# Gate steps by thirds and both all-reduces at their end, gated Wo columns on VectorE, a K row ahead of a scale part: one change to an adaLN attention block

## The chip, the cores and the metric

The kernel runs on one core of one Trainium2 chip. The metric is the device time of one execution in microseconds; lower is better. Of the kernel before there are three timed runs and one profiled execution.

## The reference

Two sequences of 256 tokens (512 rows) with 1152 channels. Everything arrives and leaves in bf16.

```python
B, N, D = (2, 256, 1152)
mod = (silu(c) @ w_mod).reshape(B, 6, 1, D)
shift_a, scale_a, gate_a = mod[:, 0], mod[:, 1], mod[:, 2]     # the other three are not used
h = layernorm(x) * (1 + scale_a) + shift_a
q, k, v = split(h @ wqkv, 3)
p = softmax(q @ k.T * D ** -0.5)                               # one head of 1152 channels
return x + gate_a * ((p @ v) @ wo)
```

## The kernel before, in words

1152 channels are nine tiles of 128 (`KT`), 512 tokens are four tiles of 128 (`TT`; two of each sequence), and most outputs are cut into chunks of 384 columns (`CW`). Weights are loaded by the SP queue in the order in which the code issues them; eight semaphores go round, so a load is issued only when the one eight places ahead of it has landed. Each engine's compute instructions run in the order in which the code calls them: the wrappers `vec`, `sca`, `ten` and `gps` record every call, and `pin` fixes that order at the end. Since the wrapper makes the call, the profile has nearly every instruction under one line, L85, and groups are told apart by the tile names. PSUM has eight banks: five called MM and one each of BA, BB and BC; `bank(..., where=...)` names one, and without `where` it takes the next of the ring.

**K, with the normalisation drawn through it.** Channels are the contraction, so x is centred (`centre`, with means from VectorE's `bn` or ScalarE's `act_mean`), transposed on TensorE (`transposes`, tile `tp`) and copied to `xcT` (`xcT_copy`). The scale of the first channel tiles comes from `scale_rows` on TensorE in three parts, PA (tiles 0 to 1), PB (2 to 4), PC (5 to 8): 9 rows of `wS` for each tile, into `psS`; `scale_open` starts each part with a matmul of ones by ones, so that the sum is 1 + scale, and `scale_out` copies it to `s1p`. `scaled` multiplies a row of `xcT` by it into `hTs`. K's nine output tiles: the first five are accumulated through all nine rows (`accs`; `k_part` and `k_step`, five matmuls a row), the other four take rows 0 and 1 in pairs (`pair_part`), are parked in SBUF (`held`) and are finished by `held_block(0)` to `held_block(3)`: seven matmuls each for rows 2 to 8 and an addition on VectorE. The inverse deviation `rstd` is made on GpSimd from the variances, spread over the partitions by a transpose and a matmul (`parts`, `pT3`, `masked`, `bc_ps`) and multiplied into all of `hTs` by VectorE (`normalised`, tile `hT`). Then the shift (`psH`, 36 matmuls in bank BB, turned into `shT`) is added to `hT` (`shifted`) by VectorE and ScalarE. The order is: `held_block(0)` and `(1)`, `psH`, `held_block(2)` and `(3)`; the last of them uses bank BB too.

**Q, scores, V.** Q takes nine rows of `wQ` (`psQ`), the scores of both sequences follow (`s_ps`), and then V in 12 groups of nine matmuls (`v_group`). The gate is not a matmul: VectorE accumulates silu(c) times `wG` in `gacc`, one partition a row of `w_mod`, in 9 steps for each sequence (`gate_steps`), first all of sequence 0 and then of sequence 1. `spread` sums over the partitions with one all-reduce on GpSimd for each sequence (`gate_bc`). VectorE makes the row maxima and the negated maxima (`scores`: `p_f`, `mx`, `nmx`), ScalarE the exponentials (`exps`), VectorE the division (`probs`, tile `pn`), and the DMA queue turns the result (`turn`, `pT`).

**Attention times V and Wo.** `pT` times `v_sb` gives `attnT`; the PSUM groups are cast by VectorE and ScalarE in turn. Then four row blocks of Wo, in chunks: VectorE multiplies a chunk by the gate (`ga`) and adds x (`o_sb`); the store follows. The last row block is cut finer. Its last 192 columns use `wo_last`, columns of Wo that GpSimd multiplied by the gate in nine steps, so that only x has to be added afterwards: by VectorE for 128 columns, and by an identity matmul on TensorE and a copy on ScalarE for the last 64.

Of the kernel before, what the change touches and what calls it, by code (L numbers as in the profile page):

```python
# [7 lines left out]
ACT = mybir.ActivationFunctionType  # L8
# [8 lines left out]
def kernel(  # L17
# [92 lines left out]
    def one(t):  # L110
        return slice(t * P, (t + 1) * P)
# [9 lines left out]
    ones_row = const.tile([1, 512], BF16)  # L121
    gps.memset(ones_row, 1.0)
# [5 lines left out]
    def mask_make():  # L128
        gps.memset(mask, 1.0)
        gps.affine_select(  # L130
            out=mask, in_=mask, compare_op=ALU.is_ge, fill=0.0, base=0,
            pattern=[[-3, TT], [0, P]], channel_multiplier=1,
        )
        gps.affine_select(
            out=mask, in_=mask, compare_op=ALU.is_ge, fill=0.0, base=2,
            pattern=[[3, TT], [0, P]], channel_multiplier=-1,
        )
# [18 lines left out]
    def load_s(part, k0, k1):  # L156
        load_mod(wS, 1, k0, k1, part[0] * P, part[1] * P)

    def load_k(k0, k1, c0=0, c1=D):
        spq.dma_start(out=wK[:, k0:k1, c0:c1], in_=wqkv_v[:, k0:k1, D + c0 : D + c1])  # L160
# [19 lines left out]
    load_k(3, 4)  # L180
    load_s(PC, 0, 4)
    load_s(PC, 4, KT)
    load_k(4, 5)
    load_k(5, 7)
# [3 lines left out]
    for k0, k1 in ((0, 2), (2, 5), (5, KT)):  # L188
        load_q(k0, k1)
# [16 lines left out]
    def silu_c():  # L206
        sca.activation(out=e_sb, in_=c_sb, func=ACT.Exp, scale=-1.0)
        gps.tensor_scalar_add(out=e_sb, in0=e_sb, scalar1=1.0)
        vec.reciprocal(out=r_sb, in_=e_sb)
        gps.tensor_tensor(out=scT_f.rearrange("p k b -> p b k"), in0=c_sb, in1=r_sb, op=ALU.mult)  # L210
        gps.tensor_copy(out=scT_rep, in_=scT_f.unsqueeze(2).to_broadcast([P, KT, NR // B, B]))
# [13 lines left out]
    def bn(t):  # L225
        st = small.tile([P, NCH, 6], F32, tag="stats", name="stats")
        for s in range(NCH):
            bn_part(t, st, s)
        mv = small.tile([P, 2], F32, tag="mv", name="mv")
        vec.bn_aggr(out=mv, in_=st)  # L230
        return mv
# [10 lines left out]
    def centre(t, scalar, op):  # L242
        vec.tensor_scalar(out=xc[:, t, :], in0=x_sb[:, t, :], scalar1=scalar, scalar2=None, op0=op)
# [11 lines left out]
    def xcT_copy(t, h, on_dve):  # L255
        k0, k1 = HALF[h]
        dst, srct = xcT[:, k0:k1, one(t)], tps[t, h][:, : k1 - k0, :]
        if on_dve:
            vec.tensor_copy(out=dst, in_=srct)
        else:  # L260
            sca.copy(out=dst, in_=srct)
# [10 lines left out]
    def scale_open(part, where):  # L272
        n = part[1] - part[0]
        ps = bank([P, n, NR], "psS", where=where)
        ten.matmul(ps.rearrange("p j r -> p (j r)"), lhsT=junk[0:1, :P], rhs=ones_row[0:1, 0 : n * NR],
                   start=True, stop=False, skip_group_check=True)
        psS[part] = ps

    def scale_rows(part, kk0, kk1, js=None):
        for j0, j1 in [part] if js is None else js:  # L280
            for kk in range(kk0, kk1):
                for j in range(j0, j1):
                    ten.matmul(psS[part][:, j - part[0], :], lhsT=wS[:, kk, j * P : (j + 1) * P], rhs=sc_rhs(kk),
                               start=False, stop=(kk == KT - 1), skip_group_check=True)

    def scale_out(part):
        vec.tensor_copy(out=s1p[:, part[0] : part[1], :], in_=psS[part][:, :, 0:B])

    def scaled(k, sl, scalar):
        vec.tensor_scalar(out=hTs[:, k, sl], in0=xcT[:, k, sl], scalar1=scalar, scalar2=None, op0=ALU.mult)  # L290

# [29 lines left out]
    def k_block(f, ps, k0, k1):  # L321
        for k in range(k0, k1):
            ten.matmul(ps, lhsT=wk(k, f), rhs=hTs[:, k, :], start=(k == k0), stop=(k == k1 - 1))
# [8 lines left out]
    silu_c()  # L332
    mask_make()
    mv0 = bn(0)
# [4 lines left out]
    scale_open(PA, BA)  # L339
# [6 lines left out]
    scale_rows(PA, 0, 4)  # L346
# [4 lines left out]
    scaled(0, tok(0), psS[PA][:, 0, 0:1])  # L351
    transposes(2, 0, BB)
    transposes(2, 1, BC)
    scale_out(PA)
    xcT_copy(2, 0, True)
    xcT_copy(2, 1, False)
    scaled(0, one(2), s1p[:, 0, 1:2])
    scaled(1, tok(0), s1p[:, 1, 0:1])
    scaled(1, one(2), s1p[:, 1, 1:2])
# [7 lines left out]
    H3 = 5 * P  # L367
# [4 lines left out]
    centre(3, nmean[:, 3:4], ALU.add)  # L372
# [9 lines left out]
    xcT_copy(3, 0, True)  # L382
    park(pr20)
    xcT_copy(3, 1, False)
    for k in range(KA):
        scaled(k, one(3), s1p[:, k, 1:2])
    st3 = small.tile([P, NCH, 6], F32, tag="stats", name="stats")
    bn_part(3, st3, 0)
    bn_part(3, st3, 1)
    for k in range(KA):  # L390
        k_part(k, one(3))
    scale_open(PB, BA)
    scale_rows(PB, 0, KT)
    scale_out(PB)
    for k in range(*PB):
        for b in range(B):
            scaled_b(k, b)
    bn_part(3, st3, 2)
    mv3 = small.tile([P, 2], F32, tag="mv", name="mv")
    vec.bn_aggr(out=mv3, in_=st3)  # L400
    mv2 = bn(2)
# [5 lines left out]
    act_var(1)  # L407
    gps.tensor_copy(out=var[:, 0:1], in_=mv0[:, 1:2])
    gps.tensor_copy(out=var[:, 3:4], in_=mv3[:, 1:2])
    gps.tensor_copy(out=var[:, 2:3], in_=mv2[:, 1:2])  # L410
    gps.tensor_scalar_add(out=rstd, in0=var, scalar1=EPS)
    gps.tensor_tensor(out=rstd, in0=rstd, in1=neg_half, op=ALU.pow)
    for k in range(PB[0], PB[1] - 1):
        k_step(k)


    scale_open(PC, BB)
    scale_rows(PC, 0, KT)
# [11 lines left out]
    k_step(PC[0] - 1)  # L430
    k_step(PC[0])
    k_step(PC[0] + 1, 0, 3)
    pT3 = bank([NP3, P], "pT3", BF16, BA)
# [3 lines left out]
    k_step(PC[0] + 1, 3)  # L437
    k_step(PC[0] + 2, 0, 2)
# [9 lines left out]
    k_step(PC[0] + 2, 2)  # L448
    for k in range(PC[0] + 3, KT):
        k_step(k)  # L450
# [3 lines left out]
    def held_block(i, where):  # L454
        ps = bank([P, T], "psK", where=where)
        k_block(NACC + i, ps, KA, KT)
        vec.tensor_tensor(out=qkT[:, KT + NACC + i, :], in0=ps, in1=held[:, i, :], op=ALU.add)

    held_block(0, BA)
    held_block(1, BC)  # L460


# [20 lines left out]
    held_block(2, MM)  # L483
    held_block(3, BB)
# [7 lines left out]
    for k0 in range(0, KT, 3):  # L492
        load_mod(wG, 2, k0, k0 + 3, 0, D)
# [6 lines left out]
    gates = [(b, kt) for b in range(B) for kt in range(KT)]  # L500
# [54 lines left out]
    def probs(b):  # L555
        rinv = small.tile([P, NQ], F32, tag="rinv")
        vec.reciprocal(out=rinv, in_=rsums[b])
        pns[b] = work.tile([P, NQ, N], BF16, tag="pn", name="pn")
        for i in range(NQ):
            vec.tensor_scalar_mul(out=pns[b][:, i, :], in0=p_fs[b][:, i, :], scalar1=rinv[:, i : i + 1])  # L560
# [19 lines left out]
    def spread(b):  # L580
        gps.partition_all_reduce(gate_bc[:, b, :], gacc[:, b, :], P, bass.bass_isa.ReduceOp.add)

    gate_steps(9)
# [3 lines left out]
    exps(1)  # L587
    probs(0)
    turn(0)
    gate_steps(1)  # L590
    probs(1)
    turn(1)
    spread(0)
    gate_steps(len(gates))
    spread(1)
# [5 lines left out]
    LASTW = 64  # L601
    TAILW = CW // 2
    wo_last = const.tile([P, KT, TAILW], BF16)
    for k in range(KT):
        gps.tensor_tensor(out=wo_last[:, k, :], in0=wO[:, k, D - TAILW :],
                          in1=gate_bc[:, B - 1, D - TAILW :], op=ALU.mult)
# [10 lines left out]

    for t in range(TT):
        b = t // NQ
        o_sb = work.tile([P, D], BF16, tag="o_sb")  # L620
        if t < TT - 1:
            chunks = [(oc * CW, CW) for oc in range(NCH)]
            dma_after = {NCH - 1: (0, D)}
        else:
            chunks = [(0, CW), (CW, CW), (2 * CW, CW - TAILW), (D - TAILW, TAILW - LASTW), (D - LASTW, LASTW)]
            dma_after = {1: (0, 2 * CW), 3: (2 * CW, CW - LASTW), 4: (D - LASTW, LASTW)}
        for ci, (c0, w_) in enumerate(chunks):
            cs = slice(c0, c0 + w_)
            last = (t == TT - 1) and (ci == len(chunks) - 1)
            pregated = (t == TT - 1) and c0 >= D - TAILW  # L630
            ps = bank([P, w_], "ps")
            if last:
                ten.matmul(ps, lhsT=ident, rhs=x_sb[:, t, cs], start=True, stop=False)
            for k in range(KT):
                ten.matmul(
                    ps, lhsT=attnT[:, k, t * P : (t + 1) * P],
                    rhs=(wo_last[:, k, c0 - (D - TAILW) : c0 - (D - TAILW) + w_] if pregated else wO[:, k, cs]),
                    start=(k == 0 and not last), stop=(k == KT - 1),
                )
            if last:  # L640
                sca.copy(out=o_sb[:, cs], in_=ps)
            elif pregated:
                vec.tensor_tensor(out=o_sb[:, cs], in0=ps, in1=x_sb[:, t, cs], op=ALU.add)
            else:
                ga = work.tile([P, CW], F32, tag="ga")
                vec.tensor_tensor(out=ga[:, :w_], in0=ps, in1=gate_bc[:, b, cs], op=ALU.mult)
                vec.tensor_tensor(out=o_sb[:, cs], in0=ga[:, :w_], in1=x_sb[:, t, cs], op=ALU.add)
            if ci in dma_after:
                d0, dw = dma_after[ci]
                dma_eng = nc.scalar if last else spq  # L650
                dma_eng.dma_start(out=out_f[t * P : (t + 1) * P, d0 : d0 + dw], in_=o_sb[:, d0 : d0 + dw])
# [36 lines left out]
```

## Time and profile before

| | |
|---|---|
| timed runs | 100.86, 101.11, 101.17 us; median 101.11 |
| profiled execution | 100.72 us, of which 98.7 is the span from first to last instruction |
| granted TensorE clock | 0.991 |
| busy | PE 90.4 (92%), DVE 78.5 (79%), ACT 31.8 (32%), POOL 27.0 (27%) |
| bytes read and written | 19.76 and 1.18 MB |
| Q's matmuls | 17.4 us busy in 32.63 to 50.10 |
| V's matmuls | 17.6 us busy in 54.10 to 71.70 |
| Wo's 99 matmuls of 384 columns | 16.3 us |

PE is TensorE, DVE is VectorE, ACT is ScalarE, POOL is GpSimd, and SP is the engine that issues most DMAs. All times in the trace are microseconds from the first instruction. A row of the timeline has its start, its duration, the engine, line and operation, the tiles written and read with their shapes, how many instructions it merges, and in brackets the idle time of the engine before it with what ended it. In the busy time by stage PE's digits can be less than the stage only where TensorE had nothing to run. Matmuls overlap, so what one costs in a row of them is the distance from start to start, which is less than its duration.

### The profile page before, as it was taken

Reading aid. Unit: us, or ns where it says so; the run is one execution under the profiler, and the core shown is the slowest. Engines: PE = TensorE matmul, PEld = TensorE weight load, DVE = VectorE, ACT = ScalarE, POOL = GpSimd, SP = SyncE. Lnnn points to the kernel's source line nnn. Section 1 sums busy time; section 2 is a strip of 40 time slices with the busy share of each in tenths; the row PEclk is TensorE's granted clock in tenths of the full one; section 3 lists DMA queues with packets and bytes.
Section 4 is the critical chain, followed back from the end, with each engine's and each line's share of the span. In section 5 each row is a group of like instructions: output and inputs, shape, how many; then the busy total and the mean of one; then the engine's idle time right before and its main releaser. Section 6 shows DMA issues by size and latency. Waiting matters only on the chain.

```text
span 98.7 us, 1694 instructions
## 1 busy us (share of the span) xinstructions
PE 90.4 (92%) x663; PEld 53.1 (54%) x667; DVE 78.5 (79%) x135; ACT 31.8 (32%) x66; POOL 27.0 (27%) x36
## 2 busy tenths in 40 slices
PE   3959999999999999999999999999996999999940
PEld 1328785633454444444468665566685655666720
DVE  1199779753999939999806999999999999879950
ACT  5288747102903700733320304832353200000000
POOL 4190000570000000000000599200003993008960
PEclk9999999999999999999999999999999999999996
DMA  1999999999999999999995000211000000330321
GB/s 32 327 316 362 381 389 393 410 411 411 408 401 412 413 410 406 372 373 383 401 414 210 0 0 0 56 33 27 0 0 0 0 0 0 121 124 0 120 80 40
DMA packets 15991, 21.31 MB, mean 216 GB/s; under 512 B 2160, under 2 KB 9328, under 8 KB 15984
## 3 DMA queue, kind: packets, MB, share of 16 engines
q1 hardware_dynamic: 15568, 21.19, 58.3%
q8 instruction: 5, 0.08, 0.4%
q10 hardware_dynamic: 416, 0.02, 0.3%
q14 instruction: 2, 0.02, 0.0%
HBM read 19.76 MB, written 1.18 MB: 212 GB/s over the span
## 4 chain that ended last, share of the span: by engine, by line
PE 25%; POOL 20%; DMA 14%; issue 14%; DVE 9%; POOLq 8%; SPq 5%; ACT 2%
PE psQ L85 18%; DMA wK<-in_wqkv_dram 14%; POOL gate_bc L85 14%; POOLq L683 7%; DVE hT L85 6%; POOL wo_last L85 6%; SPq L85 5%; PE acc L85 3%; PE s_ps L85 2%; PE psK L85 2%; DVE qkT L85 1%; ACT p_f L85 1%; DVE p_f L85 1%; DVE mx L85 1%; ACT held L85 1%
## 5 line engine op out<-in xcount | busy, mean ns | idle before, releaser
L85 POOL PARTITION_ALL_REDUCE gate_bc<-gacc x2 | 13.8, 6910 | 46.6 <-ACT p_f L85 33.4
L85 DVE SCALAR_TENSOR_TENSOR gacc<-wG,scT_f,gacc 128x1152 f32<-128x1152 bf16 x16 | 22.7, 1418 | 0.5
L85 PE MATMUL ps<-wV,hT 128*128 128x384 bf16 x108 | 17.7, 326 | 0.0
L85 PE MATMUL psQ<-hT,wQ 128*128 128x512 bf16 x80 | 17.6, 379 | 0.1
L85 PE MATMUL ps<-wO,attnT 128*128 128x384 bf16 (+1 forms) x108 | 17.0, 319 | 0.0
L85 PEld LDWEIGHTS <-attnT 128*128 128x128 bf16 x126 | 11.4, 98 | 7.1 <-issue 0.7
L85 PEld LDWEIGHTS <-hT 128*128 128x128 bf16 x108 | 10.6, 98 | 6.9
L85 PEld LDWEIGHTS <-wK 128*128 128x128 bf16 x109 | 9.4, 97 | 8.0 <-issue 1.2
L85 PEld LDWEIGHTS <-wQ 128*128 128x128 bf16 x81 | 7.9, 98 | 9.6
L85 PE MATMUL acc<-hTs,wK 128*128 128x512 bf16 (+2 forms) x63 | 11.1, 311 | 0.3 <-DMA wK<-in_wqkv_dram 0.2
L85 DVE TENSOR_TENSOR o_sb<-ga,x_sb 128x384 bf16<-128x384 f32 (+1 forms) x12 | 8.8, 735 | 0.4
L85 ACT CAST qkT<-psQ 128x512 bf16<-128x512 f32 x9 | 5.0, 592 | 12.3 <-PE psQ L85 12.3
L85 POOL TENSOR_TENSOR wo_last<-wO,gate_bc 128x192 bf16<-128x192 bf16 x9 | 6.0, 702 | 6.9 <-issue 6.9
L85 DVE TENSOR_TENSOR ga<-ps,gate_bc 128x384 f32<-128x384 f32 (+1 forms) x12 | 6.4, 537 | 1.1 <-PE ps L85 1.1
L85 ACT CAST v_sb<-ps 128x384 bf16<-128x384 f32 x12 | 5.2, 484 | 5.7 <-PE ps L85 5.7
L85 PE MATMUL psK<-hTs,wK 128*128 128x512 bf16 x27 | 6.5, 379 | 0.2
L85 DVE TENSOR_TENSOR hT<-hTs,held 128x512 bf16<-128x512 bf16 x9 | 5.5, 684 | 1.4 <-ACT held L85 1.4
L85 ACT CAST o_sb<-ps 128x64 bf16<-128x64 f32 x1 | 0.2, 213 | 18.6 <-DVE o_sb L85 18.6
L85 PE MATMUL junk_ps<-junk 128*128 128x512 bf16 x12 | 4.3, 538 | 1.5 <-DVE junk L85 1.5
L85 PE MATMUL ps<-pT,v_sb 128*128 128x256 bf16 x36 | 4.3, 272 | 0.9 <-DVE attnT L85 0.9
L85 DVE TENSOR_SCALAR nmx<-mx 128x2 f32<-128x2 f32 x2 | 4.8, 2384 | 0.1
L85 ACT ACTIVATE p_f<-p_f,nmx 128x256 f32<-128x256 f32 x4 | 2.0, 500 | 8.3 <-DVE nmx L85 8.3
(76 smaller groups left out, 90.6 us busy)
## 6 DMA issues: line engine op xcount, KB each, us to landing
wH<-in_w_mod_dram SPq DMA_DIRECT2D x3, 864.0 KB, 12.0
wG<-in_w_mod_dram SPq DMA_DIRECT2D x3, 864.0 KB, 13.9
wV<-in_wqkv_dram SPq DMA_DIRECT2D x3, 864.0 KB, 13.2
wO<-in_wo_dram SPq DMA_DIRECT2D x3, 864.0 KB, 8.7
wK<-in_wqkv_dram SPq DMA_DIRECT2D x5, 288.0 KB, 6.7
x_sb<-in_x_dram SPq DMA_DIRECT2D x4, 288.0 KB, 3.9
wK<-in_wqkv_dram SPq DMA_DIRECT2D x2, 576.0 KB, 9.1
wQ<-in_wqkv_dram SPq DMA_DIRECT2D x1, 1152.0 KB, 14.0
```

Source lines behind the costliest of these rows:

```text
L85: r = fn(*a, **k)
L683: with _tile.TileContext(nc) as tc:
```

## The change

It has these parts.

1. The six gate steps of each third of `wG` (three of each sequence) come together, 11 steps ahead of the scores, one after `exps(1)`, six after. Both all-reduces stand behind the last step, held there by an added dependency.
2. The probability division moves from VectorE to ScalarE.
3. `wo_last` moves from GpSimd to VectorE, two of its nine steps behind each chunk of Wo from the sixth on (one behind the tenth). The last row block is cut in 384, 320, 256, 128 and 64 columns; the last two are pre-gated, and both get x by an identity matmul and are copied by ScalarE.
4. K's fifth row is loaded ahead of the third scale part, rows six and seven are two loads, and Q's rows eight and nine go behind the first third of `wG`. All five of `accs` take the fifth row ahead of the third scale part; `held_block` is cut in two for block 0, so that its rows 2 to 4 lie behind that part.
5. The shift's matmuls come behind three of the four parked blocks instead of two; the last block uses bank BA.
6. The scale parts are opened by their own first matmul, and `scale_out` adds the 1. Rows 0 and 1 of the third and fourth x tile are scaled straight out of PSUM (`scaled_tp`). The fourth tile is centred in two pieces.
7. The exponential of c comes first on its engines and its reciprocal between two statistics of the first x tile. The mask is made at the start. The variance of the third x tile comes from ScalarE.

Cut to its core:

```diff
-    load_s(PC, 0, 4)
-    load_s(PC, 4, KT)
     load_k(4, 5)
-    load_k(5, 7)
+    load_s(PC, 0, 4)
+    load_s(PC, 4, KT)
+    load_k(5, 6)
+    load_k(6, 7)
     load_k(7, KT)
...
-    for k0, k1 in ((0, 2), (2, 5), (5, KT)):
+    for k0, k1 in ((0, 2), (2, 5), (5, 7)):
         load_q(k0, k1)
...
-    def scale_open(part, where):
-        n = part[1] - part[0]
-        ps = bank([P, n, NR], "psS", where=where)
-        ten.matmul(ps.rearrange("p j r -> p (j r)"), lhsT=junk[0:1, :P], rhs=ones_row[0:1, 0 : n * NR],
-                   start=True, stop=False, skip_group_check=True)
-        psS[part] = ps
...
     def scale_out(part):
-        vec.tensor_copy(out=s1p[:, part[0] : part[1], :], in_=psS[part][:, :, 0:B])
+        vec.tensor_scalar_add(out=s1p[:, part[0] : part[1], :], in0=psS[part][:, :, 0:B], scalar1=1.0)
...
+    def scaled_tp(k, t):
+        vec.tensor_scalar(out=hTs[:, k, one(t)], in0=tps[t, 0][:, k, :], scalar1=s1p[:, k, t // NQ : t // NQ + 1],
+                          scalar2=None, op0=ALU.mult)
...
+    def held_block(i, rows, where=None):
+        if where is not None:
+            psK[i] = bank([P, T], "psK", where=where)
+        for k in range(*rows):
+            ten.matmul(psK[i], lhsT=wk(k, NACC + i), rhs=hTs[:, k, :], start=(k == KA), stop=(k == KT - 1))
+
+    def add_held(i):
+        vec.tensor_tensor(out=qkT[:, KT + NACC + i, :], in0=psK[i], in1=held[:, i, :], op=ALU.add)
...
-    for k in range(PB[0], PB[1] - 1):
+    for k in range(*PB):
         k_step(k)
...
-    k_step(PC[0] - 1)
+    held_block(0, PB, BA)
     k_step(PC[0])
...
-    held_block(0, BA)
-    held_block(1, BC)
+    held_block(0, PC)
+    held_block(1, (KA, KT), BC)
+    held_block(2, (KA, KT), MM)
+    add_held(0)
+    add_held(1)
...
-    held_block(2, MM)
-    held_block(3, BB)
+    held_block(3, (KA, KT), BA)
+    add_held(2)
+    add_held(3)
...
-    for k0 in range(0, KT, 3):
-        load_mod(wG, 2, k0, k0 + 3, 0, D)
+    load_mod(wG, 2, 0, 3, 0, D)
+    load_q(7, KT)
+    load_mod(wG, 2, 3, 6, 0, D)
+    load_mod(wG, 2, 6, KT, 0, D)
...
-    gates = [(b, kt) for b in range(B) for kt in range(KT)]
+    gates = [(b, kt) for g in range(0, KT, 3) for b in range(B) for kt in range(g, g + 3)]
...
-            vec.tensor_scalar_mul(out=pns[b][:, i, :], in0=p_fs[b][:, i, :], scalar1=rinv[:, i : i + 1])
+            sca.activation(out=pns[b][:, i, :], in_=p_fs[b][:, i, :], func=ACT.Copy, scale=rinv[:, i : i + 1])
...
-    gate_steps(9)
+    gate_steps(11)
     scores(0)
     exps(0)
     scores(1)
     exps(1)
+    gate_steps(1)
     probs(0)
     turn(0)
-    gate_steps(1)
     probs(1)
     turn(1)
-    spread(0)
     gate_steps(len(gates))
-    spread(1)
+    gate_done = dve_seq[-1].ins.name
+    for b in range(B):
+        ar = gps.partition_all_reduce(gate_bc[:, b, :], gacc[:, b, :], P, bass.bass_isa.ReduceOp.add)
+        tc.add_manual_dep(ar.ins, gate_done, SYNC_SCHED, reason="keep gpsimd off the shared port")
...
-    for k in range(KT):
-        gps.tensor_tensor(out=wo_last[:, k, :], in0=wO[:, k, D - TAILW :],
-                          in1=gate_bc[:, B - 1, D - TAILW :], op=ALU.mult)
+    def gated_columns(k0, k1):
+        for k in range(k0, k1):
+            vec.tensor_tensor(out=wo_last[:, k, :], in0=wO[:, k, D - TAILW :],
+                              in1=gate_bc[:, B - 1, D - TAILW :], op=ALU.mult)
...
+            for w_ in (CW, 320, 256) + TAIL:
+                chunks.append((c0, w_))
+                c0 += w_
+            dma_after = {1: (0, chunks[2][0]), 3: (chunks[2][0], D - TAIL[-1]), 4: (D - TAIL[-1], D)}
...
-            if last:
+            if pregated:
                 sca.copy(out=o_sb[:, cs], in_=ps)
-            elif pregated:
-                vec.tensor_tensor(out=o_sb[:, cs], in0=ps, in1=x_sb[:, t, cs], op=ALU.add)
...
+                if t * NCH + ci >= 5 and todo:
+                    gated_columns(todo[0], todo[0] + 2 if len(todo) > 1 else todo[0] + 1)
+                    del todo[:2]
```

## The prediction

> **What bounds the kernel now.** I read the page first. TensorE is busy for 92% of the span and its clock is at full speed, so a gain has to come out of the other 8%, or out of what lies after the last matmul. The busy time by stage then shows where the 8% is (line by line: stage, length, PE, PEld, DVE, ACT, POOL busy with counts, clock, DMA share, GB/s).
>
> ```profile
> 8.00:20.13 12.13, 11.63 (x169) 8.68 (x171) 10.01 (x35) 6.74 (x12) 1.68 (x6) 1.00 1.06 389
> 20.13:32.63 12.50, 12.29 (x85) 5.41 (x87) 9.71 (x25) 4.44 (x10) 1.47 (x6) 1.00 1.04 408
> 32.63:50.10 17.47, 17.42 (x81) 7.93 (x81) 14.50 (x17) 5.59 (x11) 0.00 (x0) 1.00 1.06 394
> 54.10:71.70 17.60, 17.60 (x111) 10.66 (x110) 16.93 (x17) 6.84 (x19) 6.99 (x1) 1.00 0.07 16
> 71.70:76.70 5.00, 4.13 (x38) 3.50 (x37) 4.93 (x6) 2.24 (x4) 1.14 (x1) 1.00 0.00 0
> 76.70:95.90 19.20, 18.17 (x130) 11.40 (x127) 16.95 (x29) 0.59 (x1) 11.72 (x10) 1.00 0.15 57
> ```
>
> Q (its weight loads begin at 32.63) and V (54.10 to 71.70) have no hole. Holes are in three places: K up to 32.63, where the weights arrive at 390 to 410 GB/s all the time; attention times V, 0.87 us; the output projection, 1.03 us. The trace in order of time shows the last two, and the waits of GpSimd and VectorE around them:
>
> ```profile
> 55.37 6.99 POOL L85 PARTITION_ALL_REDUCE gate_bc<-gacc  x1 [33.40 <-ACT p_f L85]
> 55.90 4.60 DVE L85 TENSOR_SCALAR nmx<-mx 128x2 f32<-128x2 f32 x1
> 75.38 3.14 DVE L85 CAST attnT<-ps 128x512 bf16<-128x512 f32 x6
> 75.56 6.83 POOL L85 PARTITION_ALL_REDUCE gate_bc<-gacc  x1 [13.20 <-DVE gacc L85]
> 76.11 0.81 PE L85 MATMUL ps<-pT,v_sb 128*128 128x256 bf16 x6 [0.87 <-DVE attnT L85]
> 79.09 1.99 DVE L85 TENSOR_TENSOR o_sb<-ga,x_sb 128x384 bf16<-128x384 f32 x1
> 89.28 6.03 POOL L85 TENSOR_TENSOR wo_last<-wO,gate_bc 128x192 bf16<-128x192 bf16 x9 [6.88 <-issue]
> 94.70 0.22 PE L85 MATMUL ps<-wo_last,attnT 128*128 128x128 bf16 x1 [0.55 <-POOL wo_last L85]
> 95.36 0.22 PE L85 MATMUL ps<-wo_last,attnT 128*128 128x128 bf16 x1 [0.44 <-POOL wo_last L85]
> ```
>
> The first all-reduce, at 55.37, holds VectorE's two-element multiply (0.17 us otherwise) for 4.60 us. So the gate steps end only at 75.46, the casts of attnT come behind them, and TensorE runs out of PSUM banks. The second all-reduce ends at 82.39, GpSimd is idle for 6.88 us with no releaser, and the pre-gated Wo columns last to 95.31. That is the chain which ended last.
>
> **The K stage.** Landings are issue plus time to landing. The last piece of the third scale part lands at 18.03, K's fifth row at 18.74, rows six and seven at 20.13, eight and nine at 21.52; TensorE waits for 20.13 with the sixth row's step. After the change the fifth row stands before the scale part, so I expect the fifth row at about 14.8 (one row, 0.7 us, behind row four's 14.05) and the scale part 0.7 later, at 18.74; the split rows at 19.43 and 20.13, the rest unmoved.
> Ahead of that the VectorE chain is shorter. The reciprocal goes between two statistics, saving some 0.8 us of waiting for x's first tile; scaled rows are read straight from PSUM (an estimate of 0.19 us each between 0.16, the 128-column row from SBUF, and 0.42, the 512-column copy from PSUM); the third x tile's mean comes about 0.4 earlier; the three opening matmuls (0.20 to 0.22 each, 0.3 with their issue) are gone. Following the order of the built program with these durations, K's third row begins at 14.5 instead of 15.65. Rows three to five are 15 matmuls at 0.2155 us (the spacing of the 512-column ones), to 17.74. TensorE then stands before the scale part: 16 of its 36 rows fit before 18.74, the other 20 (0.5 us) end at 19.25. The early gain is thus eaten by the DMA. The held block's three matmuls (0.65) cover the copy of the scale and the first two scaled halves (0.20 + 0.20 + 0.28), and the sixth row starts at 19.98 instead of 20.17. What is left to Q's start: 3 matmuls fewer than before (0.65), and no wait for VectorE to release the shift's bank before the last parked block (0.28), as that block now uses another bank and lies beside the transpose of the shift. Sum 0.19 + 0.65 + 0.28 less 0.1 for the waits around the scale: Q starts at 31.66, **0.97 us earlier**.
> Next to be late would be VectorE's add of block 0 (29.55 against a need at 30.15) and, on the SP queue, Q's last two rows, now behind the gate's first third: 1.43 and 2.12 us of transfer behind 33.0 put them at 36.6; they are needed 28 matmuls after 31.66, at 37.7. Each costs nothing while these margins hold. The variance on ScalarE instead of VectorE ends its GpSimd chain at about 20.6, ahead of 21.3. The mask moves to GpSimd's idle start (2 us before c lands) at nothing.
>
> **Attention.** The all-reduces wait for the last gate step, so VectorE's multiply no longer waits 4.4 us, and the four probability multiplies (1.90 and 0.62) go to ScalarE at about 0.5 each (the exponentials' row), where only V's casts queue; those had waited until 61.53 before without stopping TensorE. Eleven gate steps fit before the scores (2 x 0.82 + 9 x 1.45 from 35.2 ends at 49.9, the scores need 51.5), one after, six more end at 65.3; the order by thirds waits for nothing that lands later than it is used. The all-reduces then take 65.3 to 72.2 and 72.2 to 79.1. The casts come free at 70.9 without a queue: TensorE gains its wait. Start to start that hole is 1.14 where 0.11 is normal: **1.03 us**. Wo starts at 74.76 instead of 76.76.
> The order against this: the second all-reduce now lies over the first chunks of Wo. In the trace an all-reduce held o_sb (two SBUF inputs, 0.56 us otherwise) so that it ended at 81.08, 5.5 us after the all-reduce began, and let the next at 81.58 pass. The first chunk's o_sb would be due at 77.1 and end at 77.7, and VectorE is level again a chunk later. [...]
>
> **The tail.** VectorE takes 1.06 us per chunk (ga to o_sb 0.59, to the next ga 0.475 when queued). The nine gated multiplies of 192 columns have o_sb's form: 0.36 us alone, 0.27 apart when queued (0.602 apart for 512 columns, 0.475 for 384). The upper bound is GpSimd's own 0.70. I take 0.27, VectorE's form. From the sixth chunk a chunk costs 1.60 against TensorE's 1.45. VectorE is 0.6 us behind when the ninth multiply is done at 91.55, before TensorE wants it at 92.0; the 320- and 256-column chunks end on VectorE at 93.4. TensorE ends at 92.4 and ScalarE's two copies at 92.95, so the store behind VectorE is last: issued 93.4, 1.65 to landing (1.62 and 1.83 for the 80 and 192 KB ones), and the 1.0 us that stood between the last landing (97.72) and the end. Before, the last store landed 2.67 later. **So the tail gives another 0.67** of the 0.99 us of waits for gated columns: the rest goes to VectorE.
>
> **Sum.** 0.97 + 1.03 + 0.67 = 2.67: span 98.7 to 96.05, the profiled execution 100.72 to 98.05. The median of the three runs is 101.11, 0.39 above the profiled one; with the same offset 98.44, say 98.4.
>
> **Rivals.**
> A. The early part gives nothing. Q starts when it did, because the scale part or K's last rows land later than I place them, or VectorE's add becomes late. For it: DMA is full there. Against: no bytes are added. 101.1 - 1.70 = 99.4.
> B. A row of transfers lands earlier: one engine's queue lay 0.9 us back behind a 16 KB instruction fetch at 15.74. If the fetch falls elsewhere, Q starts 0.5 earlier still: 97.9.
> C. Slower: the all-reduces become the bound by holding the casts too. If a cast cannot pass while one runs, TensorE's banks fill, and Wo starts after 79.1 and about 0.7 us of casts, near 79.8 instead of 74.76: 98.4 + 5.0 = 103.4. It decides as soon as Wo's start is held beyond 74.76 + 2.67 = 77.4. Against it: the six casts ran under the second all-reduce at 0.52 us each, from PSUM.
> D. The nine multiplies cost GpSimd's 0.70: nine times 0.43 is 3.9 us on a VectorE that has no slack left: 102.3. It would be slower from 0.57 each. Against: o_sb's rows.
> E. The change does not do what it says, or gives back what it gains: 101.1.
>
> **How the numbers follow.** Forecast 0.58, A 0.20, B 0.12, C 0.05, D 0.02, E 0.03. The forecast, A and B are faster; about 0.3% (0.3 us) is what a measurement can tell from no change. Low end: B with VectorE's 0.4 us in the tail not last, 97.5. High end: A with the multiplies 0.05 us dearer, 99.9; that leaves out C, D and E, and some of the odd mixtures.
>
> **What would show it.** Right: the sixth row's step at about 20.0, psQ at 31.7, no idle time of TensorE before an attnT cast, the all-reduces at 65 and 72, TensorE never waiting for wo_last, and the last store behind VectorE's o_sb. Wrong: a DMA wait of psQ at its eighth row, casts longer than 0.7 us, wo_last rows above 0.4 us, or PE waiting for ga.

## The result, and the profile after

| | before | after |
|---|---|---|
| timed runs | median 100.98 us (four, 100.84 to 101.17) | median 105.88 us (four, 105.82 to 106.67) |
| ratio | | 1.0502, 95% interval 1.0448 to 1.0556 |
| span of the profiled execution | 98.7 | 104.1 |
| busy PE, DVE, POOL | 90.4, 78.5, 27.0 | 90.6, 69.5, 20.7 |

The change is slower by 4.9 us where 2.7 us faster was forecast. VectorE and GpSimd have less to do, as intended, and TensorE as much as before; but the span has grown by 5.4 us. (Of the runs told below, two of the four of experiment 4, at 106.56 and 108.34 us, were slow ones, and its comparison leaves them out.) The busy time by stage of the changed kernel has the columns explained above:

```profile
0.00:8.00 8.00, 4.38 (x12) 1.48 (x12) 1.50 (x3) 4.36 (x8) 0.39 (x5) 1.00 0.76 228
8.00:20.00 12.00, 5.96 (x69) 5.56 (x70) 5.86 (x18) 2.88 (x6) 3.02 (x8) 0.57 1.06 391
32.00:50.00 18.00, 17.89 (x113) 8.33 (x113) 17.77 (x33) 7.29 (x16) 0.00 (x0) 1.00 1.06 394
54.00:72.00 18.00, 18.00 (x119) 11.43 (x118) 14.75 (x18) 8.13 (x22) 0.00 (x0) 1.00 0.07 17
77.00:96.00 19.00, 19.00 (x131) 12.59 (x130) 13.24 (x26) 3.30 (x6) 9.96 (x2) 1.00 0.08 32
```

From 54 us on TensorE has no hole left: the two waits that were to go have gone. All the loss stands in the first two rows: Q's weight loads begin at 39.7 instead of 32.6, and from there to the end it is 64.4 us instead of 66.1. TensorE runs only the 12 opening matmuls in the first 8 us, and in the next 12 it is busy for half the time at a mean granted clock of 0.57. The chain that ended last starts there (start, length, what; POOLq is GpSimd's sequencer, and "issue" is time in which the engine waited for nothing that the profile shows):

```profile
1.01 0.01 POOLq L85
1.02 0.02 issue
1.04 0.01 POOLq L85
1.05 8.78 issue
9.83 0.28 POOL ident L85
...
12.12 0.33 POOL e_sb L85
12.45 0.02 issue
12.47 0.27 DVE r_sb L85
12.74 0.43 DVE stats L85
...
13.46 0.53 DVE xc L85
13.99 0.04 issue
14.04 2.10 PE tp L85 x18
```

GpSimd's own rows say the same. First before, then after; only the first rows of each are shown.

```profile
0.79 0.20 POOL L85 MEMSET ident<- 128x128 bf16 x1 [0.29 <-POOLq L672]
1.28 0.29 POOL L85 TENSOR_SCALAR_AFFINE_SELECT ident<-ident 128x128 bf16<-128x128 bf16 x1 [0.29 <-POOL ident L85]
```

```profile
0.79 0.20 POOL L85 MEMSET ident<- 128x128 bf16 x1 [0.29 <-POOLq L679]
9.83 0.28 POOL L85 TENSOR_SCALAR_AFFINE_SELECT ident<-ident 128x128 bf16<-128x128 bf16 x1 [8.84 <-issue]
10.08 0.09 POOL L85 MEMSET neg_half<- 128x4 f32 x1
10.12 0.51 POOL L85 MEMSET mask<- 12x512 bf16 x1
10.70 1.33 POOL L85 TENSOR_SCALAR_AFFINE_SELECT mask<-mask 12x512 bf16<-12x512 bf16 x2
12.12 0.32 POOL L85 TENSOR_SCALAR e_sb<-e_sb 128x18 f32<-128x18 f32 x1
```

Both kernels start with the same memset and the same affine select, and both have a configuration change of GpSimd in between: a pair of sequencer instructions (MODIFY_POOL_CONFIG in the trace), at 1.18 in the trace before and at 1.01 after. Before, GpSimd is idle for 0.29 us ahead of the select; after, for 8.84, and as in the 6.88 of the old tail, nothing that the profile shows ends them. Behind the select come the mask and then the addition for the exponential of c, at 12.12 instead of 4.18. VectorE's reciprocal waits for that, the last statistics of x's first tile stand behind the reciprocal, and TensorE's first transposes start at 14.04 instead of 7.14.

What was changed at GpSimd's start stands behind that select in its order, so the other place to look is the end. Before, GpSimd's last work is the gated Wo columns, an ordinary kind, for which its configuration was changed back at 82.34. The chain of before has that pair of instructions and the stretch behind it (L683 is the end of the program; the sequencer's instruction there stood from 82.45 to 95.39, and the last multiply ended at 95.31):

```profile
75.56 6.83 POOL gate_bc L85
82.39 0.07 POOLq L85 x2
82.47 7.35 POOLq L683
89.82 5.50 POOL wo_last L85 x8
```

After, GpSimd's last work is the second all-reduce, and no change back follows it.

### The profile page after: what moved, and what is told of

The parts are those of the page before. It is cut to its first block, busy times and chain, and to the rows that moved or that the text cites. A ratio compares the mean times of both kernels' runs of the same rounds, so it can differ in the third digit from the quotient of the medians.

```text
span 104.1 us, 1684 instructions
## 1 busy us (share of the span) xinstructions
PE 90.6 (87%) x661; PEld 54.8 (53%) x665; DVE 69.5 (67%) x136; ACT 35.1 (34%) x73; POOL 20.7 (20%) x26
## 3 DMA queue, kind: packets, MB, share of 16 engines
HBM read 19.76 MB, written 1.18 MB: 201 GB/s over the span
## 4 chain that ended last, share of the span: by engine, by line
PE 74%; DVE 10%; issue 10%; POOL 2%; POOLq 0%
PE ps L85 29%; PE psQ L85 17%; PE acc L85 10%; PE psK L85 5%; PE s_ps L85 4%; PE tp L85 3%; DVE ga L85 3%; DVE o_sb L85 3%; DVE wo_last L85 2%; PE psS L85 2%; PE psE L85 2%; POOL mask L85 2%; PE psH L85 1%; DVE xc L85 1%; DVE hTs L85 0%
## 5 line engine op out<-in xcount | busy, mean ns | idle before, releaser
L85 PE MATMUL ps<-wO,attnT 128*128 128x384 bf16 (+2 forms) x108 | 17.0, 319 | 0.0
L85 PE MATMUL acc<-hTs,wK 128*128 128x512 bf16 (+2 forms) x64 | 11.6, 324 | 0.2
L85 PE MATMUL tp<-ident,xc 128*128 128x128 bf16 x36 | 4.0, 288 | 8.1 <-DVE xc L85 8.1
L85 DVE TENSOR_TENSOR ga<-ps,gate_bc 128x384 f32<-128x384 f32 (+2 forms) x12 | 6.5, 538 | 2.6 <-PE ps L85 2.6
L85 DVE CAST attnT<-ps 128x512 bf16<-128x512 f32 (+1 forms) x6 | 3.5, 603 | 6.8 <-PE ps L85 6.8
L85 PEld LDWEIGHTS <-xc 128*128 128x128 bf16 x36 | 3.3, 133 | 8.7 <-DVE xc L85 8.6
L85 DVE TENSOR_TENSOR o_sb<-ga,x_sb 128x384 bf16<-128x384 f32 (+2 forms) x12 | 6.5, 541 | 0.4
L85 ACT CAST o_sb<-ps 128x128 bf16<-128x128 f32 (+1 forms) x2 | 0.5, 238 | 17.0 <-PE ps L85 17.0
L85 ACT COPY xcT<-tp 128x640 bf16<-128x640 bf16 x4 | 2.8, 694 | 8.9 <-PE tp L85 8.9
```

The costliest lines, as they stand in the source:

```text
L85: r = fn(*a, **k)
```

## The experiments

**Theory T.** GpSimd is set either for the all-reduce or for its ordinary operations, and the idle stretch behind a configuration change (6.88 us in the tail before, 8.84 at the start after) is the swap from the first to the second. How it is set when a program ends still holds when the next execution begins. The changed kernel ends with the all-reduce, so each execution begins with a swap, and the swap that lay half hidden in the tail now lies in front of everything. That what is swapped is code, as the expectations have it, is the author's guess: no trace shows what GpSimd does in these stretches. **Rival F**: the new order of GpSimd's start makes the gap. **Rival C**: the half clock makes the loss.

**1. The swap put back at the end.**

```diff
         tc.add_manual_dep(ar.ins, gate_done, SYNC_SCHED, reason="keep gpsimd off the shared port")
+    spare = small.tile([P, TT], F32, tag="spare", name="spare")
+    gps.tensor_tensor(out=spare, in0=rstd, in1=neg_half, op=ALU.mult)
```

> The changed kernel with one thing added: behind both all-reduces GpSimd does one 128x4 multiply of its ordinary kind (into a tile that nobody reads), so that GpSimd swaps its code back before the program ends. Theory T (GpSimd keeps the all-reduce's code from one execution to the next, and the first affine select pays the swap): the gap between GpSimd's configuration change at 1.0 us and the ident select shrinks from 8.8 to under 0.5 us, Q's weight loads begin at 31.7, the granted clock never falls to a half in between, and the median is the predicted 98.4 us (97.5 to 99.9). Rival F (the new order at the start, the mask and the exponential ahead, makes the gap): nothing changes, 105.9. Rival C (the half clock from 8.2 to 18.5 us is the cause): nothing changes, 105.9.

Median 97.62 us (97.44 to 97.99) against 100.83 before on the same chip, ratio 0.9676 (0.9649 to 0.9702). One instruction of 0.34 us, whose result nobody reads, makes the changed kernel 8.3 us quicker (105.88 to 97.62). GpSimd's rows:

```profile
0.79 0.20 POOL L85 MEMSET ident<- 128x128 bf16 x1 [0.29 <-POOLq L681]
1.28 0.29 POOL L85 TENSOR_SCALAR_AFFINE_SELECT ident<-ident 128x128 bf16<-128x128 bf16 x1 [0.29 <-POOL ident L85]
...
65.44 13.69 POOL L85 PARTITION_ALL_REDUCE gate_bc<-gacc  x2 [44.69 <-DVE gacc L85]
86.67 0.34 POOL L85 TENSOR_TENSOR spare<-rstd,neg_half 128x4 f32<-128x4 f32 x1 [7.54 <-issue]
```

The idle time has moved from ahead of the affine select to ahead of `spare`, where TensorE is busy with Wo and nobody waits. Up to the all-reduces the instructions are those of the changed kernel, so the gap at the start depends on the kind of work that GpSimd does last. F is out. C is not yet: the half clock has gone together with the gap, and experiment 4 parts the two. No trace covers the time between two executions. That the setting itself stays from one to the next is the reading that fits all the kernels here; a state that is set up anew for each execution, from what the program does last, is not ruled out.

**2. The gated columns back on GpSimd.**

```diff
-            vec.tensor_tensor(out=wo_last[:, k, :], in0=wO[:, k, D - TAILW :],
+            gps.tensor_tensor(out=wo_last[:, k, :], in0=wO[:, k, D - TAILW :],
...
-    todo = list(range(KT))
+    gated_columns(0, KT)
...
-                if t * NCH + ci >= 5 and todo:
-                    gated_columns(todo[0], todo[0] + 2 if len(todo) > 1 else todo[0] + 1)
-                    del todo[:2]
```

> The changed kernel with part 3 half undone: the nine multiplies of the gated Wo columns are GpSimd's again, behind the all-reduces; all else as changed. T: the swap back lies in the tail again (all-reduces end at 79, swap 6.9, nine at 0.67: done at 92, as TensorE wants the last at 92.0); the start has no gap; VectorE loses 2.4 us in the tail but its additions are slowed beside GpSimd: 98.2 (97.6 to 99.2). F and C: 105.9 less at most 0.5 for the lighter VectorE.

Median 97.41 (97.05 to 97.88), ratio 0.9664 (0.9624 to 0.9703). That is 0.2 us below the low end, and not to be told from the first experiment (97.62). The nine multiplies run at 85.88 to 91.79 and TensorE never waits for them; VectorE is done at 92.93 instead of 93.46 in experiment 1. With useful work in place of `spare` the swap back, 6.82 us here, is free too.

**3. The kernel before, with the gated columns alone moved to VectorE.**

```diff
-    for k in range(KT):
-        gps.tensor_tensor(out=wo_last[:, k, :], in0=wO[:, k, D - TAILW :],
-                          in1=gate_bc[:, B - 1, D - TAILW :], op=ALU.mult)
+    def gated_columns(k0, k1):
+        for k in range(k0, k1):
+            vec.tensor_tensor(out=wo_last[:, k, :], in0=wO[:, k, D - TAILW :],
+                              in1=gate_bc[:, B - 1, D - TAILW :], op=ALU.mult)
+    todo = list(range(KT))
...
                 vec.tensor_tensor(out=o_sb[:, cs], in0=ga[:, :w_], in1=x_sb[:, t, cs], op=ALU.add)
+                if t * NCH + ci >= 5 and todo:
+                    gated_columns(todo[0], todo[0] + 2 if len(todo) > 1 else todo[0] + 1)
+                    del todo[:2]
```

> The kernel before with only this of the change: the gated Wo columns are multiplied by VectorE, two behind each chunk from the sixth. T: the program now ends with the all-reduce's code in GpSimd, so its start has a gap of 8 to 9 us at the first affine select although nothing at the start was touched; Q begins 6.5 to 7.5 us later than 32.6, the tail gains 0 to 0.6: 106.5 to 108.3. F: the start is as before, 100.4 to 101.0. C: the start is as before, the same 100.4 to 101.0.

Median 108.43 (107.92 to 108.75), ratio 1.075 (1.0707 to 1.0793): 0.1 above the range. An edit in the last fifth of the kernel moves its start:

```profile
0.79 0.20 POOL L85 MEMSET ident<- 128x128 bf16 x1 [0.29 <-POOLq L679]
10.90 0.28 POOL L85 TENSOR_SCALAR_AFFINE_SELECT ident<-ident 128x128 bf16<-128x128 bf16 x1 [9.91 <-issue]
```

Q's weight loads begin at 41.4 instead of 32.6, 8.8 us later (7.5 was the most expected). The gap itself was 9.91 us here, 1.1 longer than in the changed kernel. Since nothing at the start was touched, this excludes F a second time.

**4. Opening matmuls that bridge the gap.**

```diff
-    fillers(12)
+    fillers(40)
```

> The changed kernel with 40 opening matmuls on junk instead of 12, so that TensorE is busy to about 13 to 14 us. T: the gap of 8.8 us stays; only the half clock behind it goes, in which TensorE worked from 14.0 to 18.5 at half rate: 1 to 2.2 us better, 103.7 to 104.9. C: if the clock is the cause, it is back near 99 to 101. F: as T.

104.27 and 104.95 us, about 104.6, ratio 1.0375 (1.0324 to 1.0426). The gap stays (9.57 us) and the clock no longer falls. First the changed kernel, then this one:

```profile
8.20:18.40 10.20, 4.36 (x50) 4.09 (x51) 4.85 (x15) 2.17 (x4) 3.02 (x8) 0.50 1.06 389
```

```profile
8.00:18.40 10.40, 8.35 (x84) 5.29 (x82) 4.88 (x16) 2.91 (x6) 3.02 (x8) 1.00 1.07 393
```

From the first transposes to Q's weight loads it is 38.83 - 14.77 = 24.06 us, and 39.69 - 14.04 = 25.65 in the changed kernel. So the half clock is 1.6 us of the loss, not its cause, and C is out; some of the 1.6 is lost again in a longer gap.

**5. Attention alone.** The kernel before with the gate by thirds, both all-reduces behind the last step, and the probabilities on ScalarE; the edit is those hunks of the change's diff. GpSimd keeps the gated columns.

> The kernel before with parts 1 and 2 alone: gate steps by thirds, both all-reduces behind the last step, probabilities on ScalarE. K, the loads and the tail are as before, the gated columns stay on GpSimd. By the terms of the prediction's sum: the wait for attnT goes (1.03 us), and since the all-reduces end at 80, the swap back 6.9 later and the nine multiplies at 92.9, TensorE's waits for the gated columns (0.99) shrink to 0.1 or less although part 3 is not there: 98.8 (98.4 to 99.4). If part 3 was what removed those waits: 99.8.

Median 98.82 (98.65 to 98.98), ratio 0.9804 (0.9779 to 0.983). TensorE's waits have only the opening and the first transposes left:

```profile
PE junk_ps L85 <- DVE junk L85: 1.5, 1, 1.5
PE tp L85 <- DVE xc L85: 1.0, 2, 0.8
```

The multiplies stand at 87.45 to 93.02 and TensorE takes them as they come. So two of the forecast's gains, the wait for attnT and those for the gated columns, need no part 3.

**6 and 7. K's order of before, and the reference beside it.** Run 6 is experiment 2 with the loads, `k_step`, `held_block` and banks of before; run 7 is experiment 2 again on the same chip.

```diff
-    load_k(4, 5)
     load_s(PC, 0, 4)
     load_s(PC, 4, KT)
-    load_k(5, 6)
-    load_k(6, 7)
+    load_k(4, 5)
+    load_k(5, 7)
...
-    for k in range(*PB):
+    for k in range(PB[0], PB[1] - 1):
         k_step(k)
...
-    held_block(0, PB, BA)
+    k_step(PC[0] - 1)
...
-    held_block(3, (KA, KT), BA)
+    held_block(2, (KA, KT), MM)
+    held_block(3, (KA, KT), BB)
```

> The changed kernel with GpSimd's gated columns and with parts 4 and 5 undone: loads, K's rows around the third scale part and the four parked blocks in the order of before. Parts 6 and 7 stay. By the sum (0.65 for three matmuls ahead of the scale part's landing and 0.28 for the bank): Q begins 0.9 later than in the kernel with the new order, 32.7 instead of 31.8, and the time is 0.7 to 1.0 us above it. Rival (the gain in K comes from the quicker start, parts 6 and 7): Q begins at 31.8 here too, and the time is the same within 0.2.

> The changed kernel with GpSimd's gated columns once more, beside the last on the same chip: 97.4 (97.0 to 97.8), 3.0 to 3.6% below the kernel before.

Medians 97.98 (97.7 to 98.26) and 97.45 (97.25 to 97.62), ratios 0.9721 (0.9696 to 0.9746) and 0.9669 (0.9644 to 0.9694). The new order is worth 0.53 us, between the two answers. Q's weight loads begin at 31.9 and 31.3; TensorE's waits for the third scale part, first in the old order, then in the new, show a part of it:

```profile
17.62 0.67 PE L85 MATMUL psS<-scT_rep,wS 128*128 128x32 bf16 x20 [0.75 <-DMA wS<-in_w_mod_dram]
```

```profile
18.41 0.67 PE L85 MATMUL psS<-scT_rep,wS 128*128 128x32 bf16 x20 [0.53 <-DMA wS<-in_w_mod_dram]
```

The scale part comes 0.79 us later when a K row goes ahead of it, and one row's five matmuls, 1.08 us, are done by then: 0.29 us gained. Where the rest of the 0.53 comes from was not taken apart. The kernel of experiments 2 and 7 has the lowest medians of the study.

## Why the prediction was wrong

**The step that failed** is the tail's, where the nine multiplies were moved off GpSimd and priced by what they cost VectorE. The 6.88 us of idle time ahead of them was quoted in the first part, called idle "with no releaser", and then dropped from the sum together with the multiplies. By the runs it was the swap back to ordinary operations, which each execution paid once, in the tail or at the start; on the chain of before it is the 7.35 us of POOLq ahead of the multiplies. With its last ordinary GpSimd work gone, the swap went to the first affine select, 8.84 us at the start of the changed kernel. The prediction walked through every queue within one execution and never asked in which state it leaves the engine to the next. None of its rivals has this step: E ("gives back what it gains") leaves room for it, without a mechanism and at 101.1, and C and D, which forecast a slower kernel (103.4 and 102.3), do so for other reasons.

In the traces the price of a swap is 6.8 to 7.7 us in the tail and 8.8 to 9.9 at the start, with no instruction to show for it (the releaser is "issue" in each). That the price moves to the program's start when nothing pays it in the tail is what the runs here showed.

A second step fails with it: "The mask moves to GpSimd's idle start (2 us before c lands) at nothing". The cover was the wait for c, and with the swap there is no such wait: the mask and its selects stand from 10.12 to 12.03 between the select and the addition that everything waits for.

**The rest of the sum held.** It can be read in experiment 1, which has all parts of the change and no swap at the start. In the changed kernel itself, from Q's weight loads to the end it is 104.1 - 39.7 = 64.4 us; in experiment 1, 96.3 - 31.9 = 64.4; before, 98.7 - 32.6 = 66.1. So attention and tail together gave the 1.7 us that was forecast for them (1.03 and 0.67), and Q begins 0.77 us earlier in experiment 1 (32.63 to 31.86) where 0.97 was forecast.

| step | forecast | measured in experiment 1 |
|---|---|---|
| Q begins | 31.66 | 31.9 (31.8 and 31.3 in 2 and 7) |
| all-reduces | 65.3 to 79.1 | 65.4 to 79.1 |
| Wo's first matmul | 74.76 | 75.0 |
| wait for attnT | gone | gone |
| gated multiplies on VectorE | 0.27 apart | 0.27 apart (0.62 for two, the last 0.35 long) |
| VectorE's last addition ends | 93.4 | 93.46 |
| span | 96.05 | 96.3 |
| time | 98.4 | 97.6 |

The time is 0.8 us below the forecast although the span is 0.2 above it: 1.7 us lie outside the span in that execution (97.99 against 96.3), where 2.0 were carried over from before, and the median lies 0.37 below the profiled execution, where the forecast put it 0.39 above. The changed kernel begins Q 39.7 - 31.9 = 7.8 us later than experiment 1, and 96.05 + 7.8 is its span of 104.1 within 0.3.

Where the terms were right and the credit wrong: the tail's 0.67 was put down to part 3, and experiment 5 shows that TensorE's waits for the gated columns vanish with parts 1 and 2 already, as the all-reduces end earlier. From Q's weight loads to the end it is 64.5 us in experiment 5, 64.4 in experiment 1 and 64.1 in experiment 2: the move of the multiplies to VectorE gave nothing, and that the tail's 0.67 came out was luck as far as part 3 goes. In K the quicker start was said to be eaten by the DMA, 0.19 us left and 0.93 for the order. By the runs the order is worth 0.53, and Q begins 0.6 us earlier in run 6 than in run 5 with parts 6 and 7.

The prediction's rival C (casts held by the all-reduces) is out: in experiment 1 the six casts run from 71.67 to 75.59, under both all-reduces, at their usual durations (0.69 at most, 0.68 before). Its D is out by the 0.27, and its A by Q's start. Its B is open: the same kernel began Q at 31.8 in experiment 2 and at 31.3 in experiment 7, as far apart as B's 0.5; where the instruction fetch that B names lay in them was not shown, and no run moved the fetch alone.

The second all-reduce, which now lies over the first chunks of Wo, held none of VectorE's additions there. In experiment 1 the first chunk's o_sb, with two SBUF inputs, ran in its usual 0.56 us while the second all-reduce, from 72.21 to 79.13, still had 1.8 us to go:

```profile
77.29 0.56 DVE L85 TENSOR_TENSOR o_sb<-ga,x_sb 128x384 bf16<-128x384 f32 x1
```

In the trace before, the o_sb that was held ended 5.5 us after the all-reduce's begin; the same distance would be 77.7 here, and this one ended at 77.85.

## What to carry to other kernels

When work is taken off an engine, look at what its last instruction leaves behind. In these runs the kind of GpSimd's last work was such a state: the swap that disappeared from the tail (6.88 us) reappeared at the start (8.84). An idle time that the profile lets nobody end is a cost whose owner must be found before it is struck from a sum; here the configuration change stood just ahead of it on the chain, and one of the same kind at 1.2 us had only 0.29 us of idle time behind it in the kernel that swapped in its tail. If GpSimd has all-reduces and ordinary operations to do, put the swap back where nobody waits: here one tiny ordinary operation behind the last all-reduce turned 5% slower into 3% faster (ratios 1.0502 and 0.9676).

## What the runs showed of the hardware that was not expected

- In these runs what GpSimd did last decided its gap at the start. Kernels whose last GpSimd work is ordinary (before, 1, 2, 5) have 0.29 us of idle time ahead of their first affine select; those that end on the all-reduce (after, 3, 4) have 8.84, 9.91 and 9.57 us. The memset ahead of it ran at 0.79 in all seven and did not wait for the swap. The change the other way cost nothing that the trace shows: GpSimd's configuration was changed for the all-reduces at 21.91 before and at 29.35 after, in an idle stretch of 33 and 44 us, and the first all-reduce began within 0.25 us of the end of what it waited for.
- The same swap took 6.8 to 7.7 us in the tail and 8.8 to 9.9 at the start, where the weights come in at 228 to 391 GB/s (57 GB/s in the tail of before). Whether the traffic lengthens it was not tried.
- In the changed kernel's hole of 8.1 us without a matmul the granted clock of TensorE fell to 0.50 at 8.2, and stayed there until 18.4, 4.4 us into its new work. This was worth 1.6 us, less than the hole that caused it.
